# An earlier due time for the unit work that the eighth job's lists need

## The chip, the core and the metric

The kernel runs on one core of a Trainium2 chip. The metric is the device time in microseconds: the median of three runs, and beside it one execution taken by the hardware profiler. Engines are named as in the profile: PE is TensorE (PEld its weight loads), DVE is VectorE, ACT is ScalarE, POOL is GpSimd and SP is SyncE, which here only issues DMAs.

## What is computed

A gated recurrence runs along 4 sequences of 3648 steps with 256 channels, and a two-level mixture of experts with 16 experts (4 groups of 4) is applied to its 14592 output rows. Every row goes to exactly one expert.

```python
f = lower_bound + (1 - lower_bound) * sigmoid(f_logit)
h[t] = f[t] * h[t-1] + (1 - f[t]) * x[t]          # rows of h are the tokens
g = argmax(h @ w_group);  e = argmax(h @ w_expert[g])
out[row] = g_w * e_w * (relu(h[row] @ w1[g, e]) @ w2[g, e])   # 256 -> 1024 -> 256
```

`g_w` and `e_w` are the softmax weights of the chosen group and expert.

## The kernel before

**Units.** The rows are cut into 29 units of 512. A unit is loaded as one transfer (1 MB; on ScalarE's queue from unit 12 on, `p1_load`), goes through tanh and an affine map on ScalarE (`p1_ta`), a gate and two scans on VectorE (`p1_tb`), is transposed to row form on TensorE and copied out by ScalarE (`p1_back`), and its router products are made (`p1_router`, `p1_logits`). Units 8 to 27 are routed in groups of two: `route_thunks` finds each row's expert and place, and eight indirect DMAs on POOL scatter the group's rows to a list per expert in HBM (`xs`, line 393).

**Jobs.** Expert work comes as 32 jobs, numbered from 0 here. Job k (0 to 15, kind A) takes the first 2 to 5 blocks of 128 rows of an expert that is chosen while units are still being made: `EARLY[k]` says from which unit on (its cut) and how many blocks, and `choose` and `place` pick the expert and the rows' place. The eighth job is job 7, `EARLY[7] = (14, 3)`: 384 rows, from the lists as they stand when units 0 to 13 are in. Jobs 16 to 31 take what is left. The first four (`RAW = 4`) use the fp32 weights as loaded and work out their own output at once; later jobs split each weight piece into an fp16 and a bf16 part (a cast on ScalarE, line 971, and a difference on VectorE, line 973), and a job's second product stands behind the next job's first.

**Loads of a job.** Four weight pieces of 512 KB come on SyncE's queue (`job_weights`), up to eight staging buffers ahead; the rows come by `job_rows` (line 946), also on SyncE, and must wait until the scatters of all units before the cut have landed. `early_rows(u)` puts down the row loads of the jobs with cut u. SyncE works strictly in program order.

**What sets the order.** The work on units is a list of 577 small pieces, `thunks`. Job steps are written out one after the other, and after each step `bg_step` puts down as many pieces as a rate says. A step is a block of the first product or a part of the second: 10 per job for jobs 0 to 5, 19 for jobs 6 and 7, 20 for jobs 8 to 10. `due` holds pairs: by this step, this many pieces. The rate is the largest, over the open pairs, of pieces missing by steps left. The pair for job mi + 2 falls in the middle of job mi, so that of job 7 (piece 334, where `early_rows(14)` has been put down) falls in the middle of job 5, at step 55. SyncE, TensorE, VectorE and ScalarE are held to the order in which this is written, apart from what a scheduling layer moves within it; POOL's order is that layer's. In the functions below `thunks` come from `p1_thunks`, `macros` are the jobs, `marks[u]` is the number of pieces up to `early_rows(u)`.

Of the kernel before, what the change touches and what calls it, by code (L numbers as in the profile page):

```python
# [22 lines left out]
EARLY = [(4, 2), (6, 2), (8, 2), (8, 2), (10, 2), (10, 2), (12, 3), (14, 3),  # L23
         (16, 4), (18, 4), (20, 4), (22, 5), (24, 5), (26, 5), (28, 5), (28, 5)]
# [11 lines left out]
RAW = 4  # L36
# [17 lines left out]
def gated_scan_moe(ctx: ExitStack, tc, zx, lower, wroute, wexp, out, S):  # L54
# [785 lines left out]
    def make_job(kind, idx):  # L840
        j = Job()
        j.kind, j.idx = kind, idx
        j.len = EARLY[idx][1] * P if kind == "A" else CAPS[idx] if kind == "B" else P
        j.tiles = -(-j.len // P)
        j.chunks, j.pieces, j.cols, j.parts = [], [], [], []
        at = 0
        while at < j.len:
            rest = j.len - at
            if kind == "B":
                w = rest if rest <= UNIT else UNIT if rest >= UNIT + P else UNIT - P  # L850
            else:
                w = 2 * P if rest > 3 * P else P if rest > 2 * P else rest
            n = UNIT // w
            j.cols.append([list(range(c, min(KF, c + n))) for c in range(0, KF, n)])
            j.pieces += [(b, min(2 * P, at + w - b)) for b in range(at, at + w, 2 * P)]
            parts, b = [], at
            while b < at + w:
                m = at + w - b
                g = 1 if m > 64 else 2
                parts.append((b, min(m, P // g), g))  # L860
                b += P // g
            j.chunks.append((at, w))
            j.parts.append(parts)
            at += w
        j.raw = kind == "A" and idx < RAW
        j.wh, j.wl, j.st = {}, {}, {}
        j.hh, j.hl = {}, {}
        j.xh, j.xl = {}, {}
        return j
# [279 lines left out]
    macros = [[make_job("A", e)] for e in range(NE)]  # L1149
# [17 lines left out]
    def first_parts():  # L1167
        out = []
        for (j,), u in zip(macros, PLAN):
            half = {}  # L1170

            def begin(j=j, half=half):
                half[0] = bank("m2")
                raw2(j, 0, 0, range(KF // 2), half[0])
            fs = [lambda j=j: job_xt(j, 0)]
            fs += [lambda j=j, cs=cs: m1_step(j, 0, cs) for cs in j.cols[0]]
            fs += [begin, lambda j=j, half=half: m2_step(j, 0, 0, half[0])]
            out += [(u, f) for f in fs]
        return out

    thunks, marks = p1_thunks(list(range(NU)), GROUPS, first_parts())
# [56 lines left out]
    def work(mac):  # L1238
        return sum(len(j.chunks) * KF + sum(len(p) for p in j.parts) for j in mac)

    due = []
    at = 0
    for mi, mac in enumerate(macros):
        at += work(mac)
        if mi + 2 < len(macros):
            nxt = macros[mi + 2][0]
            due.append((at - (work(mac) // 2 if mi else 0), marks[EARLY[nxt.idx][0]] if nxt.kind == "A" else marks["order"]))
            if nxt.kind == "A" and nxt.idx >= NE - 2:
                due[-1] = (at - work(mac) // 2, marks["order"])
    now = [sum(work(mac) for mac in macros[:len(PLAN)])]  # L1250
    credit = [0.0]

# [110 lines left out]
```

## Time and profile before

| what | value |
|---|---|
| median of three runs | 763.11 us (760.62 to 766.0) |
| profiled execution | 761.96 us |
| its span, first to last instruction | 760.2 us |
| mean granted TensorE clock | 0.994 |
| TensorE busy | 715.6 us, 94% |
| VectorE busy | 514.6 us, 68% |
| ScalarE busy | 445.9 us, 59% |
| POOL busy | 296.3 us, 39% |
| bytes moved by DMA | 151.35 MB, 199 GB/s on average |

The shares are averages over stages that have different limits, so the stretch of the jobs in question is read from the views by window. A busy TensorE is not one at its peak. A wait is put down to the engine that released it last. A record of a queue (SPq, ACTq) is the issue of a DMA, not its transfer.

### The profile page before, as it was taken

Reading aid. Unit: us, or ns where it says so; the run is one execution under the profiler, and the core shown is the slowest. Engines: PE = TensorE matmul, PEld = TensorE weight load, DVE = VectorE, ACT = ScalarE, POOL = GpSimd, SP = SyncE. Lnnn points to the kernel's source line nnn. Section 1 sums busy time; section 2 is a strip of 40 time slices with the busy share of each in tenths; the row PEclk is TensorE's granted clock in tenths of the full one; section 3 lists DMA queues with packets and bytes.
Section 4 is the critical chain, followed back from the end, with each engine's and each line's share of the span. In section 5 each row is a group of like instructions: output and inputs, shape, how many; then the busy total and the mean of one; then the engine's idle time right before and its main releaser. Section 6 shows DMA issues by size and latency. Waiting matters only on the chain.

```text
span 760.2 us, 17863 instructions
## 1 busy us (share of the span) xinstructions
PE 715.6 (94%) x6471; PEld 588.0 (77%) x6471; DVE 514.6 (68%) x1086; ACT 445.9 (59%) x827; POOL 296.3 (39%) x314
## 2 busy tenths in 40 slices
PE   3569999998899999999999999999999999999995
PEld 1457888886788888888999676867778886777895
DVE  6899758999799976495556754644644645755660
ACT  6567767887577855454545644544544545655651
POOL 3656267668567764632222121312122121123232
PEclk9999999999999999999999999999999999999998
DMA  8978789989888873657994470617155345655520
GB/s 326 413 255 292 243 351 289 408 316 310 289 258 292 242 211 117 170 146 189 222 241 106 113 189 29 169 43 188 47 155 131 114 133 168 196 174 170 168 65 23
DMA packets 100410, 151.35 MB, mean 199 GB/s; under 512 B 60203, under 2 KB 70206, under 8 KB 97504
## 3 DMA queue, kind: packets, MB, share of 16 engines
q1 hardware_dynamic: 85792, 102.84, 46.1%
q0 software_dynamic: 11408, 30.02, 10.7%
q10 hardware_dynamic: 3120, 17.34, 6.7%
q8 instruction: 51, 0.84, 0.5%
q14 instruction: 39, 0.32, 0.1%
HBM read 112.49 MB, written 37.96 MB: 198 GB/s over the span
## 4 chain that ended last, share of the span: by engine, by line
PE 71%; DVE 11%; issue 8%; DMA 3%; POOL 3%; ACT 2%; another core or an unknown queue 1%; SPq 1%; POOLq 0%; DVEq 0%
PE ps_m L1129 28%; PE ps_m L1099 7%; PE ps_m L1097 7%; PE ps_m L1098 7%; PE ps_m L1110 4%; PE ps_m L1071 4%; PE ps_p L1097 3%; PE ps_p L1098 3%; PE ps_p L1099 3%; PE ps_p L284 3%; POOL out_dram L1143 3%; DVE h L256 2%; DVE w L973 1%; PE ps_p L303 1%; DVE hl L1103 1%
## 5 line engine op out<-in xcount | busy, mean ns | idle before, releaser
L1129 PE MATMUL ps_m<-w,hh 128*128 128x256 f16 (+5 forms) x1260 | 218.9, 268 | 1.3 <-issue 1.3
L1129 PE MATMUL ps_m<-w,hl 128*128 128x256 f16 (+4 forms) x740 | 188.5, 267 | 0.6 <-issue 0.6
L973 DVE TENSOR_TENSOR w<-st,w 128x1024 bf16<-128x1024 f32 x112 | 135.8, 1219 | 68.2 <-ACT w L971 66.7
L393 POOL DMA_INDIRECT xs<-rows,posi x114 | 138.2, 1212 | 87.6 <-ACT rows L288 25.6
L1143 POOL DMA_INDIRECT out_dram<-o,info x67 | 71.6, 1069 | 244.1 <-ACT o L1141 226.6
L1129 PE MATMUL ps_m<-w,rows 128*128 128x256 f16 (+5 forms) x880 | 133.8, 267 | 0.3 <-issue 0.3
L1129 PEld LDWEIGHTS <-hh 128*128 128x128 f16 (+7 forms) x1260 | 117.9, 101 | 15.6 <-issue 3.3
L971 ACT CAST w<-st 128x1024 f16<-128x1024 f32 x112 | 116.1, 1047 | 17.6 <-PE ps_m L1129 12.5
L1097 PE MATMUL ps_m<-xh,w 128*128 128x256 f16 (+9 forms) x494 | 120.4, 256 | 2.5 <-DVE hl L1103 2.4
L1099 PE MATMUL ps_m<-xh,w 128*128 128x256 f16 (+9 forms) x494 | 120.3, 256 | 0.8 <-issue 0.8
L1098 PE MATMUL ps_m<-xl,w 128*128 128x256 bf16 (+9 forms) x494 | 120.3, 256 | 0.0
L1103 DVE SCALAR_TENSOR_TENSOR hl<-ps_m,hh 128x512 bf16<-128x512 f32 (+7 forms) x107 | 71.1, 671 | 40.6 <-ACT hh L1102 24.7
L1098 PEld LDWEIGHTS <-w 128*128 128x128 f16 x800 | 78.3, 98 | 25.3 <-issue 3.7
L1097 PEld LDWEIGHTS <-w 128*128 128x128 f16 x800 | 78.3, 98 | 23.2 <-issue 1.6
L1099 PEld LDWEIGHTS <-w 128*128 128x128 bf16 x800 | 78.3, 98 | 22.8 <-issue 0.4
L1143 POOL DMA_INDIRECT out_dram<-o,meta x47 | 53.4, 1136 | 101.8 <-ACT o L1141 69.1
L1129 PEld LDWEIGHTS <-rows 128*128 128x128 f16 (+4 forms) x880 | 81.6, 101 | 10.0 <-issue 0.6
L1102 ACT ACTIVATE hh<-ps_m 128x512 f16<-128x512 f32 (+7 forms) x107 | 63.3, 594 | 37.1 <-PE ps_m L1099 32.1
L1141 ACT ACTIVATE o<-ps_m,info 128x256 f32<-128x256 f32 (+4 forms) x67 | 31.1, 463 | 91.5 <-PE ps_m L1129 75.8
L1129 PEld LDWEIGHTS <-hl 128*128 128x128 bf16 (+4 forms) x740 | 70.8, 101 | 9.1 <-issue 1.9
L256 DVE TENSOR_TENSOR_SCAN h<-zt,h 128x512 f32<-128x512 f32 (+3 forms) x48 | 56.6, 1191 | 0.5
L1103 DVE SCALAR_TENSOR_TENSOR hh<-ps_p,rows 128x512 bf16<-128x512 f32 (+7 forms) x30 | 17.6, 586 | 45.4 <-ACT rows L1102 45.3
(203 smaller groups left out, 1183.4 us busy)
## 6 DMA issues: line engine op xcount, KB each, us to landing
st<-in_wexp_dram SPq DMA_DIRECT2D x112, 512.0 KB
zt<-in_zx_dram ACTq DMA_DIRECT2D x16, 1024.0 KB
w<-in_wexp_dram SPq DMA_DIRECT2D x16, 512.0 KB
xs<-blank SPq DMA_DIRECT2D x26, 258.0 KB
zt<-in_zx_dram SPq DMA_DIRECT2D x6, 1024.0 KB
st<-in_zx_dram SPq DMA_DIRECT2D x8, 512.0 KB
xr<-xs SPq DMA_DIRECT2D x12, 258.0 KB
xr<-xs SPq DMA_DIRECT2D x16, 129.0 KB
```

The source lines that it names most:

```text
L256: sn = nc.vector.tensor_tensor_scan(out=h[:, k, c0 - a:c1 - a], data0=ff[:, k, c0 - a:c1 - a], data1=uu[:, k, c0 - a:c1 - a], initial=init ...
L393: sc = nc.gpsimd.indirect_dma_start(out=xs_v[G["t0"] + t][:, :], out_offset=bass.IndirectOffsetOnAxis(ap=R["posi"][:, t:t + 1], axis=0), i ...
L971: nc.scalar.copy(j.wh[i], j.st[i])
L973: nc.vector.tensor_tensor(out=j.wl[i], in0=j.st[i], in1=j.wh[i], op=ALU.subtract)
L1097: nc.tensor.matmul(po, w1_at(j.wh, k, c), xh[:, k], start=(k == 0), stop=False)
L1098: nc.tensor.matmul(po, w1_at(j.wh, k, c), xl[:, k], start=False, stop=False)
L1099: nc.tensor.matmul(po, w1_at(j.wl, k, c), xh[:, k], start=False, stop=(k == KD - 1))
L1102: eviction[0] = nc.scalar.activation(hi, pv, AF.Relu).ins
L1103: nc.vector.scalar_tensor_tensor(out=h_at(j.hl[ch], cs, slice(0, w)), in0=pv, scalar=0.0, in1=hi, op0=ALU.max, op1=ALU.subtract)
L1129: nc.tensor.matmul(pm[i * q:i * q + n, 0:dw], h_at(h[ch], [c], ts)[:, 0], w2_at(w, c)[:, i * dw:(i + 1) * dw], start=(c == 0 and s == 0), ...
L1141: nc.scalar.activation(o[s, 0:dw], pm[s, 0:dw], AF.Copy, scale=lt.bitcast(F32)[s, r, 1:2])
L1143: nc.gpsimd.indirect_dma_start(out=out_v[out_n[0]].rearrange("n (g d) -> (n g) d", g=g), out_offset=bass.IndirectOffsetOnAxis(ap=lt[s, r, ...
```

## The change

One line is added behind the loop that fills `due`: the pieces up to `early_rows(14)` (piece 334) are to be put down by the last step of job 3, step 40, and no longer by step 55.

```diff
             if nxt.kind == "A" and nxt.idx >= NE - 2:
                 due[-1] = (at - work(mac) // 2, marks["order"])
+    due.append((sum(work(mac) for mac in macros[:RAW]), marks[EARLY[RAW + 3][0]]))
     now = [sum(work(mac) for mac in macros[:len(PLAN)])]
```

No other pair is changed. Going through `bg_step` with the two lists gives the pieces put down by the end of each job (two units with their routing are 34 pieces):

| end of job | 0 | 1 | 2 | 3 | 4 | 5 | 6 | 7 | 8 | 9 | 10 |
|---|---|---|---|---|---|---|---|---|---|---|---|
| before | 210 | 247 | 279 | 301 | 319 | 341 | 380 | 415 | 450 | 484 | 515 |
| with the change | 212 | 252 | 293 | 334 | 346 | 362 | 392 | 422 | 454 | 485 | 515 |

The instructions themselves stay the same; their order on the engines moves. On SyncE before, at the row loads of job 7 (`posA_2055` is the place of its rows, the two `xr` loads are its rows; the two `st` loads ahead of them are the second and third weight piece of job 8):

```order
L963 DMA st_2210<-in_wexp_dram 128x1024
L963 ISA
L963 DMA st_2215<-in_wexp_dram 128x1024
L896 ISA
L896 TENSOR_LOAD posA_2055
L896 ISA x2
L946 ISA
L946 REGISTER_ALU
L946 DMA xr_2321<-xs 128x258
L946 ISA
L946 DMA xr_2323<-xs 128x516
```

With the change, the same two loads (now `posA_1952`, `xr_2126`, `xr_2128`) stand directly behind the choice of job 8's expert (`who_1922`), which follows the third weight piece of job 6; `st_2147` is the fourth piece of job 6:

```order
L661 TENSOR_LOAD who_1922
L661 ISA x2
L896 ISA
L896 TENSOR_LOAD posA_1952
L896 ISA x2
L946 ISA
L946 REGISTER_ALU
L946 DMA xr_2126<-xs 128x258
L946 ISA
L946 DMA xr_2128<-xs 128x516
L963 ISA
L963 DMA st_2147<-in_wexp_dram 128x1024
```

So these row loads moved ahead of eight weight loads. On POOL before, around the scatters of units 12 and 13 (`posi_1897`; the two `out_0_dram` rows are job 3's output, and the bookkeeping of units 14 and 15 begins at `sel_2383`):

```order
L393 DMA xs<-rows_1518,posi_1897 248832x258 x3
L1143 DMA out_0_dram<-o_1908,xr_1228 14592x256
L1143 DMA out_0_dram<-o_1938,xr_1228 14592x256
L393 DMA xs<-rows_1518,posi_1897 248832x258
L393 DMA xs<-rows_1651,posi_1897 248832x258 x4
L674 TENSOR_SCALAR sel_2383<-fill_2368,top_2370 128x16
L677 TENSOR_SCALAR gone_2385<-sel_2383 128x16
L393 DMA xs<-rows_1793,posi_2279 248832x258
```

With the change the scatters of units 12 and 13 read `posi_1854`, and the bookkeeping of units 14 and 15 (`sel_2211` and the four rows after it) and job 3's output stand as follows:

```order
L393 DMA xs<-rows_1506,posi_1854 248832x258 x4
L393 DMA xs<-rows_1636,posi_1854 248832x258 x2
L674 TENSOR_SCALAR sel_2211<-fill_2196,top_2198 128x16
L711 TENSOR_TENSOR got_2258<-got_2258,sel_1933 128x16
L677 TENSOR_SCALAR gone_2213<-sel_2211 128x16
L712 TENSOR_TENSOR taken_94<-taken_94,got_2258 128x16
L678 TENSOR_TENSOR least_96<-least_96,gone_2213 128x16
L393 DMA xs<-rows_1636,posi_1854 248832x258 x2
L1143 DMA out_0_dram<-o_2062,xr_1228 14592x256
L1143 DMA out_0_dram<-o_2089,xr_1228 14592x256
```

The last two of these scatters now stand behind that bookkeeping, and job 3's output stands behind all eight. Between job 1's second output write and the eighth of these scatters there are 19 scatters, 2 output writes and 3 such groups of bookkeeping; between job 1's second output and job 3's first there were 14 scatters before.

## Rows read from the trace of the kernel before

**Rows 1.** Busy time by stretch, all engines; the first line names the columns.

```profile
core 0: us, PE busy (x) PEld busy (x) DVE busy (x) ACT busy (x) POOL busy (x), PEclk, DMA share, GB/s
...
101.50:120.00 18.50, 18.50 (x129) 15.46 (x128) 11.81 (x26) 13.28 (x27) 12.45 (x13) 1.00 0.81 285
120.00:136.80 16.80, 16.80 (x103) 14.40 (x102) 13.67 (x32) 13.86 (x26) 11.74 (x16) 1.00 1.01 341
...
136.80:160.00 23.20, 23.20 (x260) 20.42 (x258) 23.10 (x49) 19.55 (x36) 12.30 (x11) 1.00 1.02 400
160.00:215.00 55.00, 48.96 (x507) 40.42 (x504) 49.16 (x99) 40.01 (x78) 41.33 (x42) 1.00 0.91 292
215.00:270.00 55.00, 53.84 (x535) 47.61 (x533) 54.23 (x105) 41.90 (x82) 40.34 (x39) 1.00 0.81 259
270.00:700.00 430.00, 428.08 (x3757) 344.67 (x3756) 254.33 (x494) 224.05 (x393) 110.69 (x109) 1.00 0.54 148
```

**Rows 2.** Waits of TensorE, 60 to 270 us: total, times, longest, in us.

```profile
PE ps_m L1097 <- DVE hl L1103: 2.1, 3, 1.0
PE ps_m L1129 <- issue: 1.9, 7, 0.4
PE ps_p L284 <- DVE both L381: 1.3, 1, 1.3
```

**Rows 3.** Timeline of TensorE: start, us, engine, line, operation.

```profile
101.50 0.59 PE L1071 MATMUL ps_m<-xh,w 128*128 128x256 f32 x2
...
103.23 0.60 PE L284 MATMUL ps_p<-ident,h 128*128 128x128 f32 x4
...
136.79 0.27 PE L1097 MATMUL ps_m<-xh,w 128*128 128x256 f16 x1
```

**Rows 4.** Groups of instructions on VectorE, 101.5 to 270 us: busy us, mean ns.

```profile
L256 DVE TENSOR_TENSOR_SCAN h<-zt,h 128x512 f32<-128x512 f32 (+3 forms) x30 | 34.0, 1140 | 0.2
...
L245 DVE SCALAR_TENSOR_TENSOR zt<-zt 128x1024 f32<-128x1024 f32 (+1 forms) x15 | 17.7, 1180 | 5.6 <-ACT zt L229 5.6
```

**Rows 5.** Timeline of VectorE, 155 to 175 us.

```profile
156.48 0.18 DVE L381 TENSOR_TENSOR both<-ps_p,both 128x32 f32<-128x32 f32 x1
...
159.62 1.28 DVE L256 TENSOR_TENSOR_SCAN h<-zt,h 128x512 f32<-128x512 f32 x1
...
167.91 0.31 DVE L330 TENSOR_REDUCE mx<-Lg 128x40 f32<-128x160 f32 x1
...
170.44 0.67 DVE L1103 SCALAR_TENSOR_TENSOR hl<-ps_m,hh 128x512 bf16<-128x512 f32 x1
```

**Rows 6.** POOL, the scatter group: 101.5 to 120 us, then 120 to 136.8 us.

```profile
L393 POOL DMA_INDIRECT xs<-rows,posi x8 | 8.5, 1058 | 5.7 <-DVE rows L375 2.0 <-issue 1.9 <-ACT rs L308 1.8
...
L393 POOL DMA_INDIRECT xs<-rows,posi x6 | 9.1, 1512 | 3.3 <-ACT rs L308 1.3 <-issue 0.9 <-DVE rows L375 0.8
```

**Rows 7.** Timeline of POOL, 100 to 160 us.

```profile
103.08 0.98 POOL L1143 DMA_INDIRECT out_dram<-o,xr  x1 [0.30 <-issue]
...
129.06 2.01 POOL L393 DMA_INDIRECT xs<-rows,posi  x1 [0.30 <-issue]
...
131.99 0.33 POOL L674 TENSOR_SCALAR sel<-fill,top 128x16 f32<-128x16 f32 x1 [0.91 <-DVE got L706]
...
133.92 1.81 POOL L393 DMA_INDIRECT xs<-rows,posi  x1 [0.81 <-DVE rows L375]
...
153.56 1.04 POOL L393 DMA_INDIRECT xs<-rows,posi  x1 [1.01 <-ACT rows L286]
```

**Rows 8.** Timeline of SyncE's DMA issues, 130 to 165 us.

```profile
137.41 0.93 SPq L946 DMA_DIRECT2D xr<-xs  x2
...
138.71 15.41 SPq L963 DMA_DIRECT2D st<-in_wexp_dram  x8
...
162.01 0.93 SPq L946 DMA_DIRECT2D xr<-xs  x2
```

**Rows 9.** Timeline of ScalarE, 148 to 156 us.

```profile
150.80 2.00 ACT L971 CAST w<-st 128x1024 f16<-128x1024 f32 x2
```

## The prediction

> **What bounds the kernel now.** I read the busy time by stretch first [rows 1]. From 101.5 to 160 us TensorE is busy all the time, from 160 to 215 it is idle for 6.0 us, from 215 to 270 for 1.2, and from 270 to 700 for 1.9 of 430. The granted clock is 1.00 in all stretches from 101.5 on, the higher of its two levels, so nothing is to be won or lost there. A change that only reorders work, and is back in step with the old order by the end of job 10, can win what TensorE waits in between: at most 6.0 + 1.2 = 7.2 us, 0.9% of the kernel.
>
> Who ends those waits is the second view [rows 2]: the largest are VectorE's (`hl` 2.1 us, `both` 1.3), and 1.9 us have no releaser that the trace shows. So behind the idle TensorE stands a full VectorE: busy 23.1 of 23.2 us from 136.8 to 160 and 54.2 of 55 from 215 to 270, while from 101.5 to 136.8 it has 11.8 + 13.7 = 25.5 of 35.3, 9.8 us free [rows 1]. That stretch is jobs 2 and 3: job 2's first product starts at 101.50, job 4's at 136.79 [rows 3]. The DMA engines are the other thing to look at: their share is 0.81, 1.01 and 1.02 in the three stretches from 101.5 to 160 [rows 1].
>
> **The change, part by part.** It adds one due time and no work. Emitting runs 5 pieces ahead of the old order at the end of job 1, 33 at the end of job 3, 21 after job 5, 12 after job 6, 7 after job 7 and none after job 10 (the table in the section on the change). Two units with their routing are 34 pieces, so the change carries nearly one group of two units out of jobs 4 to 10 and into the jobs before, 28 of 33 pieces into jobs 2 and 3. What a group costs:
>
> VectorE: per unit a gate of 1.18 us and two scans of 1.14, 3.46, twice 6.9 [rows 4]. Routing up to the running count goes from 167.91 to 170.44, 2.5 us; from there to the positions from 156.48 to 159.62, 3.1 less the one scan in it, 2.0 [rows 5]. Together 11.4 us; 28/34 of it is 9.4.
>
> TensorE: four transposes of `h` take 0.60 us as recorded [rows 3]; a unit has two such rows and the router's products, which I count as a third: 1.8, twice 3.6, on the high side since recorded ends overlap. It goes onto the path of jobs 2 and 3 and off it later, so it is zero in the sum, but those jobs end 28/34 of it, 3.0 us, later, at about 139.8.
>
> POOL: eight scatters, each 1.06 to 1.51 us and 0.30 of issue, 10.9 to 14.5 us [rows 6, 7].
>
> Do they fit in 35.3 + 3.0 = 38.3 us? VectorE needs 25.5 + 9.4 = 34.9, and has 3.4 left. POOL has 24.2 busy in 28 instructions [rows 1], with 0.30 each 32.6, and is given 28/34 of 10.9 to 14.5, that is 9.0 to 11.9: 41.6 to 44.5. POOL alone doesn't fit, by 3 to 6 us. VectorE at 91% in an in-order queue isn't safe either: where it is busy 49.2 of 55 us, from 160 to 215, TensorE waits for 6.0; where it is full, from 136.8 to 160, for nothing. So the new waits of TensorE in jobs 2 and 3 are between 0 and 4.2 (6.0 us in 55, over 38.3). I take 1.5, nearer to the stretch that lies beside it.
>
> The relief behind: VectorE sheds 12, 9, 5 and 3 pieces in jobs 4 and 5, 6, 7 and 8, at 11.4/34 = 0.34 us each 4.0, 3.0, 1.7 and 1.0. The first lies ahead of the waits, which begin with job 6 (161 us), and shortens the queue that VectorE enters it with. What this gives back is between 0 and 7.2 us; I take 3.5, half, because the waits of `both` are of TensorE and VectorE on one another, which a shorter queue does not shorten.
>
> What is moved past what, on SyncE. Row loads of job 7 now stand before the fourth weight piece of job 6 and all of job 7; before, they stood behind the third piece of job 8. SyncE is in order, so whatever keeps these row loads back keeps the weights back. They wait for the last scatter of units 12 and 13. In the order on POOL 19 scatters, three bookkeeping groups and two output writes lie between job 1's second write (start 103.08) and that scatter, and two of the scatters stand behind the bookkeeping of units 14 and 15, which needs VectorE's list of that group. From 104.1: 19 times 1.36 to 1.81, 25.8 to 34.4; two writes of 1.3; three groups of 1.1 (from 131.99 to the next scatter at 133.92, less its wait of 0.81) [rows 6, 7]: 135.8 to 144.4, and POOL's waits come on top (0.81 to 1.01 where the rows show one). I take 144. From a scatter's end to the row loads that wait for it the old trace has 6.3 us (131.07 to 137.41) and 7.4 (154.60 to 162.01), both under a full DMA; with fewer weights under way it can be shorter, above nothing. Row loads 144 to 151.4, weights 1.3 later (137.41 to 138.71) [rows 8]. The piece is 512 KB, at 400 GB/s 1.3 us, and at most as long as a scatter's 7.4: there at 146.6 to 160.1. It was used at 151.8, the second of the two casts from 150.80 [rows 9]; moved by the 3.0, less what job 4 no longer carries (6 pieces at 3.6/34, 0.6), at 154.2. So between 7.6 us early and 5.9 late; ScalarE would stand at the cast, and the evictions behind it that free TensorE's banks. I take 1.0.
>
> POOL's price is where a rule bears on it. The scatter group's mean is 1.06 us where VectorE is busy 11.8 of 18.5 us and 1.51 where it is busy 13.7 of 16.8 [rows 1, 6]. The Trainium skill, page "SBUF — State Buffer", section "Who interferes with whom", says that GpSimd and VectorE share one port pair as an exclusive lock, held for a whole instruction, and that VectorE instructions with two SBUF inputs contend with GpSimd's reads; that speaks against putting gates and splits beside scatters. By that rule the 19 scatters would all cost 1.51 us, the row loads would come near the late end, and the sum would have 5.9 where it has 1.0, 765.9; the trace agrees in direction, with two rows, and shows no mechanism.
>
> **Sum.** The profiled execution took 761.96 us (span 760.2 and 1.76 around it). 761.96 + 1.5 + 1.0 - 3.5 = 760.96. It lies 1.15 under the median 763.11 of the runs shown; against that the same sum gives 762.1. I forecast 761.5, between them.
>
> **Rivals.** A: as summed, a small shift that nearly cancels. For it: no engine gets less work in all, and TensorE works through the stretch either way.
>
> B: the shift empties VectorE's queue ahead of jobs 6 to 9 and all 7.2 us go, nothing new comes: 763.11 - 7.2 = 755.9. For it: the waits are VectorE's; against it: 1.9 of them are nobody's, and VectorE still holds over 90% of the stretch.
>
> C, on the other side: SyncE is held at job 7's row loads and job 6's fourth weight piece comes late. It decides from the point where the piece lands after 154.2: with a landing of 1.3 us that is a release of the row loads after 151.6, with one of 7.4 already after 145.5. Place: the casts of job 6, then job 7's pieces right behind. Price: 5.9 late for job 6, with nothing won back, 763.1 + 5.9 = 769.0; with 1.3 more for job 7's first piece behind it 770.3. For it: POOL doesn't fit, and the prefetch of eight staging buffers stands empty meanwhile; against it: the DMA engines are less full then, and the middle of the bounds is in time.
>
> D: nothing moves because TensorE hides it all: 763. For it: TensorE's zero idle from 101.5 to 160.
>
> **How the numbers follow.** A 0.45, B 0.18, C 0.25, D 0.12. About 1%, 7.6 us, is what a measurement of this kernel can tell from no change. Faster by more than that needs more than B holds in waits, so a third of B: 0.05. Slower needs C near its late end together with waits in jobs 2 and 3 (up to 4.2): half of C, 0.12. Within: 0.83. The range goes from B, 755.5, to C, 769.5; some 0.13 lies above it and 0.06 below.
>
> **What would show it.** In the changed kernel's trace: SyncE's two row loads of job 7 at 145 to 153, and then its weights, where the old trace has a run of eight weight issues from 138.71 on; a DMA share from 138 to 150 clearly under 1.0; POOL without gaps from 104 to 150; VectorE about 90% busy from 101.5 to 139.8. Right in A: TensorE's idle from 160 to 270 falls to about 4 us and 1 to 2 us of it appear before 140. Wrong if ScalarE waits for a weight load at job 6's casts by more than 3 us (C), if TensorE's waits from 160 on stay at 7 (no relief), or if anything behind job 10 differs by more than 1 us.

## The result, and the profile of the changed kernel

The change made the kernel slower by 1.4%: 774.08 us (median of six, 771.92 to 775.91) against 762.98 for the kernel before on the same chip, a ratio of 1.014 with a 95% interval of 1.0106 to 1.0174. That is 11.1 us, outside the range that was given. The profiled execution took 772.6 us, its span 770.8.

Busy time by stretch in the changed kernel, with the columns of [rows 1]:

```profile
core 0: us, PE busy (x) PEld busy (x) DVE busy (x) ACT busy (x) POOL busy (x), PEclk, DMA share, GB/s
101.50:136.80 35.30, 35.30 (x244) 29.33 (x243) 28.19 (x63) 26.02 (x52) 26.82 (x29) 1.00 0.90 305
136.80:160.00 23.20, 18.57 (x147) 14.68 (x146) 16.71 (x36) 14.53 (x28) 18.17 (x17) 0.85 0.86 301
160.00:215.00 55.00, 50.85 (x519) 43.47 (x517) 51.32 (x107) 41.95 (x79) 29.13 (x31) 0.97 0.90 314
215.00:270.00 55.00, 53.05 (x524) 46.45 (x522) 52.72 (x99) 43.48 (x80) 43.54 (x39) 1.00 0.86 274
270.00:700.00 430.00, 428.14 (x3773) 345.40 (x3776) 252.81 (x490) 221.84 (x389) 114.11 (x112) 1.00 0.53 146
```

From 101.5 to 136.8 TensorE is full, as in [rows 1]. The loss is in the second row: from 136.8 to 160, where TensorE had no idle time before, it is now idle for 4.6 us, and the granted clock is 0.85 of its upper level. From 160 to 270 it is idle for 6.1 us (before 7.2), so the relief that was to come there is 1.1 us. Behind 270 nothing moved: 428.14 busy against 428.08.

TensorE's waits from 101.5 to 215 us (total, times, longest), and its timeline around the largest:

```profile
PE ps_m L1129 <- ACT hh L1102: 3.8, 1, 3.8
PE ps_m L1097 <- DVE hl L1103: 2.9, 2, 1.9
```

```profile
148.32 0.64 PE L1033 MATMUL ps_p<-ident,xr 128*128 128x128 f32 x4
152.76 1.04 PE L1129 MATMUL ps_m<-w,hh 128*128 128x256 f16 x4 [3.80 <-ACT hh L1102]
153.58 0.42 PE L1097 MATMUL ps_m<-xh,w 128*128 128x256 f16 x1
```

TensorE waits 3.8 us for the first eviction of job 4's first product, that is for ScalarE to copy it out of TensorE's accumulators (`hh`). Behind the wait a matmul of 256 columns takes 0.42 us where [rows 3] has 0.27: the clock has fallen to 1.2 GHz. Why the eviction is late stands in ScalarE's timeline, and in the chain of work that ended last (start, us, what):

```profile
139.99 0.34 ACTq L205 DMA_DIRECT2D zt<-in_zx_dram  x1
140.37 1.06 ACT L219 ACTIVATE zt<-zt 128x1024 f32<-128x1024 f32 x1 [3.00 <-DMA st<-in_wexp_dram]
...
151.16 1.06 ACT L219 ACTIVATE zt<-zt 128x1024 f32<-128x1024 f32 x1 [4.59 <-DMA zt<-in_zx_dram]
152.12 0.58 ACT L1102 ACTIVATE hh<-ps_m 128x512 f16<-128x512 f32 x1
```

```profile
129.47 10.50 DMA st<-in_wexp_dram
...
139.99 11.15 DMA zt<-in_zx_dram
```

ScalarE stands for 4.59 us at the tanh of unit 19, whose load of 1 MB was issued at 139.99 and landed 11.15 us later; the eviction is the next instruction in its queue. The issue itself had waited for the landing of a weight piece that took 10.50 us. So the chain that sets the end goes through 21.65 us of transfers in a row, where that of the kernel before stays on TensorE until 147.76. SyncE's DMA issues in the same time, and the share of the DMA engines from 130 to 160 us:

```profile
139.38 2.13 SPq L963 DMA_DIRECT2D st<-in_wexp_dram  x4
156.83 1.05 SPq L946 DMA_DIRECT2D xr<-xs  x2
158.15 0.33 SPq L963 DMA_DIRECT2D st<-in_wexp_dram  x1
```

```profile
130.00:140.00 10.00, 10.00 (x67) 8.55 (x66) 9.73 (x27) 5.18 (x11) 7.57 (x8) 1.00 0.98 283
140.00:150.00 10.00, 8.13 (x74) 6.46 (x72) 6.54 (x19) 5.46 (x12) 7.40 (x9) 1.00 0.99 349
150.00:160.00 10.00, 7.24 (x42) 5.69 (x43) 7.21 (x11) 8.84 (x15) 8.17 (x7) 0.66 0.71 255
...
101.50:146.06 44.56, 43.73 (x314) 36.10 (x313) 33.86 (x83) 31.23 (x64) 33.04 (x35) 1.00 0.91 304
151.60:158.40 6.80, 5.64 (x27) 4.24 (x28) 4.95 (x6) 6.80 (x11) 5.58 (x5) 0.50 0.65 242
```

SyncE is held at job 7's row loads until 156.83, as rival C had it, and issues no weight from 141.5 to 158. But the DMA engines are full without it until 150. Full does not mean that they move as much. In the kernel before the same stretches are:

```profile
130.00:140.00 10.00, 10.00 (x75) 8.52 (x74) 8.73 (x24) 8.40 (x16) 7.67 (x9) 1.00 1.01 402
140.00:150.00 10.00, 10.00 (x104) 8.84 (x102) 9.90 (x18) 8.11 (x15) 5.89 (x6) 1.00 1.03 409
...
101.50:136.52 35.02, 35.02 (x227) 29.59 (x226) 25.20 (x58) 26.86 (x52) 23.91 (x28) 1.00 0.91 311
```

By the clock the changed kernel moves no more bytes here but fewer: 10.8 MB from 101.5 to 136.8 us (before 11.0) and 7.0 MB from there to 160 (before 9.3), each the rate times the time. What has grown is what had moved by a given place in the program: the second product of job 3 ends at 146.06 and not at 136.52, and from 101.5 to that place 13.5 MB moved and not 10.9.

The span grew by 10.6 us (770.8 for 760.2). The rows account for about 8.0 of them: 4.6 of idle time up to 160, 2.8 because 5.64 busy us ran at half the clock from 151.6 to 158.4, 1.7 at a clock of 0.97 from 160 to 215, less the relief of 1.1. The rest was not followed.

### The profile page after: what moved, and what is told of

Its sections match the earlier page's. It is cut to its first block, busy times and chain, and to the rows that moved or that the text cites. A ratio compares the mean times of both kernels' runs of the same rounds, so it can differ in the third digit from the quotient of the medians.

```text
span 770.8 us, 17856 instructions
## 1 busy us (share of the span) xinstructions
PE 719.2 (93%) x6467; PEld 589.4 (76%) x6471; DVE 515.9 (67%) x1086; ACT 447.1 (58%) x827; POOL 300.5 (39%) x314
## 3 DMA queue, kind: packets, MB, share of 16 engines
q0 software_dynamic: 11408, 30.02, 10.6%
## 4 chain that ended last, share of the span: by engine, by line
PE 61%; issue 13%; DVE 11%; DMA 5%; POOL 4%; ACT 3%; SPq 1%; another core or an unknown queue 1%; POOLq 0%; ACTq 0%; DVEq 0%
PE ps_m L1129 26%; PE ps_m L1099 7%; PE ps_m L1097 6%; PE ps_m L1098 6%; POOL out_dram L1143 4%; PE ps_m L1110 3%; DVE w L973 3%; PE ps_p L1099 3%; PE ps_p L1097 2%; DMA zt<-in_zx_dram 2%; PE ps_p L1098 2%; DVE h L256 2%; PE ps_m L1071 2%; PE ps_p L284 2%; DVE hl L1103 2%
## 5 line engine op out<-in xcount | busy, mean ns | idle before, releaser
L1097 PE MATMUL ps_m<-xh,w 128*128 128x256 f16 (+9 forms) x494 | 122.3, 259 | 5.8 <-DVE hl L1103 3.5
L1099 PE MATMUL ps_m<-xh,w 128*128 128x256 f16 (+9 forms) x494 | 122.2, 259 | 0.1
L1098 PE MATMUL ps_m<-xl,w 128*128 128x256 bf16 (+9 forms) x494 | 122.2, 259 | 0.1
```

Of the source, the lines that this page charges most:

```text
L1097: nc.tensor.matmul(po, w1_at(j.wh, k, c), xh[:, k], start=(k == 0), stop=False)
L1098: nc.tensor.matmul(po, w1_at(j.wh, k, c), xl[:, k], start=False, stop=False)
L1099: nc.tensor.matmul(po, w1_at(j.wl, k, c), xh[:, k], start=False, stop=(k == KD - 1))
```

## Experiments

The runs were taken on several chips, so each is held against the kernel before on its own chip (751.8 to 762.5 us there); ratios have 95% intervals. Names that begin with e_ and a_ are the changed kernel with an edit, names with b_ the kernel before with one.

### Four single waits: e_swap, e_warm, e_rows, e_load

The trace suggests four single causes, and each run takes one away.

**e_swap**: the tanh of unit 19 behind job 4's second eviction.

```diff
-(p1_load(u + AHEAD - 1), u + 1 in us and p1_ta(u + 1))
+(p1_load(u + AHEAD - 1), u + 1 in us and (later.append(u + 1) if u + 1 == 19 else p1_ta(u + 1)))
 def bg_step(q, left, n):
+    if later and now[0] + n >= 44:
+        with tc.issue_after(eviction[0]):
+            p1_ta(later.pop())
```

> The changed kernel, but the tanh of unit 19, which waits 4.6 us on ScalarE for its load at 151.16 us, is put behind the second eviction of job 4's first product, not ahead of the first. No work changes, and no load. Theory L (this one wait on ScalarE's in-order queue, with job 4's evictions behind it, is the loss, together with the clock that falls behind it): TensorE's wait of 3.8 us before 152.76 goes, and the half clock of 151.6 to 158.4 with it (about 3.4 us), so about 774.1 - 7 = 767. Theory S (SyncE is held at job 7's row loads and weights come late): the weights are as late as before, 773 to 775. Theory F (VectorE, GpSimd and the DMA engines are simply overfull there): the wait moves to the next eviction or to VectorE, 772 to 775.

**e_warm**: 64 idle matmuls in TensorE's gap, behind the third block of job 4's first product.

```diff
+if j.kind == "A" and j.idx == RAW and cs[0] == 4:
+    with tc.issue_after(mm.ins):
+        warmed[0] = keep_warm(bank("m2"), 64)
```

> The changed kernel with 64 matmuls of 128 columns whose result nobody reads, put on TensorE into the gap of 3.8 us behind the third first product of job 4. They take some 3.5 to 4 us at the higher clock where TensorE stood idle. This asks how much of the loss is the clock. If the fall of the granted clock behind the gap is a price of its own: the clock stays at 1.00 from 151 to 158, and 774.1 - 3.4 = 770.7. If something else (evictions, VectorE, loads) binds in that stretch: the clock stays up, and the time stays at 773 to 775. If the matmuls outlast the gap: up to 1 us longer.

**e_rows**: job 7's row loads back in SyncE's queue where they stood before.

```diff
 def early_rows(u):
+    if u == EARLY[RAW + 3][0] and now[0] < 56:
+        later.append(u)
+        return
...
 now[0] += n
+if later and now[0] >= 56:
+    early_rows(later.pop())
```

> The changed kernel, but job 7's two row loads are put into SyncE's queue at the place in job 5 at which they stood before the change; the units and everything else stay as early as the change has them. Theory S (rival C of the prediction: SyncE held at the row loads, weights behind them late): weights flow from 140 us on, and the most of the 11 us goes, 763 to 767. Theory L (the late load ahead of tanh on ScalarE): that load comes no sooner, since more weights now share the DMA engines with it; the wait of 4 to 5 us at tanh stays, 772 to 776.

**e_load**: the loads of z and x most of a unit earlier.

```diff
-seq += [lambda u=u: p1_back(u - 1, 0)]
+seq += [lambda u=u: (p1_back(u - 1, 0), p1_load(u + AHEAD))]
```

> The changed kernel, but each unit's load of z and x on ScalarE's queue is issued most of a unit earlier (behind the first copy of the unit two before in place of one step later); same bytes, same buffers. Theory L: the loads land ahead of their tanh, ScalarE's wait of 4.6 us goes with TensorE's 3.8 and the clock's fall, 766 to 769. Theory F (the DMA engines are full, so an earlier load makes another one late): weights or row loads come later by as much, 771 to 775. Theory S: nothing of SyncE's order changes, 772 to 775.

| kernel | us | ratio to the kernel before |
|---|---|---|
| changed kernel | 774.08 | 1.0140 (1.0106 to 1.0174) |
| e_swap | 772.96 | 1.0139 (1.0075 to 1.0203) |
| e_warm | 775.96 | 1.0174 (1.0112 to 1.0236) |
| e_rows | 772.11 | 1.0142 (1.0092 to 1.0192) |
| e_load | 779.99 | 1.0262 (1.0200 to 1.0323) |

None brings back anything that these intervals can tell, and e_load costs 1.2% more. (In e_load 172 of VectorE's and 97 of TensorE's rows moved too, so that price is not the loads' alone.) The waits of TensorE in e_swap, 101.5 to 215 us, show why:

```profile
PE ps_p L316 <- ACT w L973: 2.4, 1, 2.4
PE ps_p L303 <- ACT rows L286: 1.6, 1, 1.6
PE ps_m L1112 <- ACT hl L1076: 1.3, 1, 1.3
```

The 3.8 us are gone and three other waits, 5.3 us together, have come. In e_warm the stretch from 136.8 to 160 keeps the full clock, and TensorE still has 3.95 us without work, beside the 64 matmuls that do nothing:

```profile
136.80:160.00 23.20, 19.25 (x206) 15.92 (x205) 16.80 (x35) 14.96 (x28) 16.68 (x17) 1.00 0.83 289
```

So the fallen clock is not what binds there. In e_rows SyncE issues twelve weights from 137.24 on with no row load between them, and ScalarE waits for the same load a little longer than in the changed kernel:

```profile
137.24 34.90 SPq L966 DMA_DIRECT2D st<-in_wexp_dram  x12
...
150.50 1.06 ACT L219 ACTIVATE zt<-zt 128x1024 f32<-128x1024 f32 x1 [5.64 <-DMA zt<-in_zx_dram]
```

That is the end of rival C (theory S): SyncE was held as it says, and its release is worth nothing that can be told. Theory L falls too, as far as it names one wait. Where each wait that goes is replaced by another, a resource that all of them share may be short. Theory D: the DMA engines are full there, and the change asks for the loads, scatters and row loads of about two units earlier. Theory E, against it: the order of the work on the engines, which the change moves as well.

### Bytes alone: b_dma, b_dma1, b_dmalate

The kernel before, with copies of 1 MB that nobody reads on SyncE's queue: three in jobs 2 and 3 (b_dma, below), one there (b_dma1: at step 28 alone), or three in jobs 11 and 12 (b_dmalate: at steps 158, 174 and 190). In b_dma and b_dma1 the order of every engine but SyncE stays as it was up to 400 us; in b_dmalate 77 of VectorE's and 45 of ScalarE's rows move, from 330 us on. SyncE runs ahead of the other engines: the copies of b_dma were issued at 95.90, 120.14 and 136.59 us.

```diff
 now[0] += n
+for k, at in enumerate((22, 28, 34)):
+    if now[0] - n < at <= now[0]:
+        sync.dma_start(out=idle[k * P:(k + 1) * P, 0:2048], in_=zx[k * P:(k + 1) * P, :])
```

> The kernel before, with three copies of 1 MB from zx to a scratch tensor that nobody reads, put into SyncE's queue in jobs 2 and 3 (3 MB, about what the change carries into the stretch: two loads of z and x, and eight scatters). No engine gets any work. Theory D (the DMA engines are full from 120 to 200 us, so traffic put there ahead of its time makes everything behind it late): 3 MB at the 300 to 400 GB/s of that stretch are 7.5 to 10 us, so 762 + 7 to 10 = 769 to 772, and TensorE's idle appears from 140 us on. Theory E (what counts is the order of work on VectorE, ScalarE and GpSimd): 762 to 764.

> The kernel before with one copy of 1 MB, in the middle of jobs 2 and 3, in place of three. Theory D with no room left: a third of the 8.0 us, 2.7, so 765. Theory D with some room before it binds: less than 1 us, 762 to 763.5.

> The kernel before with the same three copies of 1 MB to a scratch tensor, but put into SyncE's queue in jobs 11 and 12 (about 270 to 340 us), where the DMA engines' share is 0.55. Theory D (the stretch is full, the bytes cost because they stand there): nothing, 762 to 763.5. If such copies cost wherever they stand (by SyncE's queue or the landing that later loads wait for): 766 to 771, as in jobs 2 and 3.

| kernel | us | before, same chip | ratio |
|---|---|---|---|
| b_dma, 3 MB in jobs 2 and 3 | 770.52 | 762.50 | 1.0105 (1.0081 to 1.0129) |
| b_dma1, 1 MB there | 761.68 | 756.91 | 1.0067 (1.0039 to 1.0095) |
| b_dmalate, 3 MB in jobs 11 and 12 | 757.23 | 756.91 | 1.0001 (0.9973 to 1.0029) |

3 MB of copies with no work for any engine cost the kernel before 8.0 us, within the 7 to 10 that theory D gave. A single copy costs 0.67%, 4.8 us and not a third of 8 (its interval goes from 3 to 7), so there was no room at that place. The same 3 MB cost nothing later, where the kernel before has a DMA share of 0.54. ScalarE's timeline and a stretch of b_dma:

```profile
129.44 1.04 ACT L972 CAST w<-st 128x1024 f16<-128x1024 f32 x1 [2.68 <-DMA st<-in_wexp_dram]
...
139.80 1.04 ACT L972 CAST w<-st 128x1024 f16<-128x1024 f32 x1 [1.08 <-DMA st<-in_wexp_dram]
142.87 1.05 ACT L972 CAST w<-st 128x1024 f16<-128x1024 f32 x1 [1.17 <-DMA st<-in_wexp_dram]
```

```profile
101.50:136.80 35.30, 33.38 (x217) 27.95 (x216) 25.37 (x59) 24.31 (x48) 22.52 (x27) 1.00 0.96 327
```

Here it is the weights that come late, and TensorE is idle for 1.9 us already before 136.8. The copies stand on SyncE's own queue, ahead of these weights, while the loads and scatters that the change moves are issued by ScalarE and POOL. So the runs show what 3 MB cost at this place, and not that the change's own transfers cost it in the same way.

### Half the change: e_half

```diff
-due.append((sum(work(mac) for mac in macros[:RAW]), marks[EARLY[RAW + 3][0]]))
+due.append((sum(work(mac) for mac in macros[:RAW]), marks[EARLY[RAW + 3][0]] - 16))
```

> The change at half its size: the same due place, 16 pieces fewer (318 of the pieces by the end of the first four jobs, where the kernel before has 301 and the changed one 334). Theory D: half the traffic is moved, 5 us of the 11: 766 to 769. If the loss comes from a point that is passed only near the full size (one load that comes later than its reader): 761 to 765.

770.60 us, 1.0095 (1.0071 to 1.0120): with 17 of the 33 pieces moved, two thirds of the loss and a little more than the 766 to 769 us of theory D. The loss does not come only near the full size.

### Bytes taken away: a_halfw and b_halfw, a_quart and b_quart

Both kernels without every second weight load of jobs 4 to 7 (4 MB), or with the first of four alone (6 MB less); the splits are kept. Up to 400 us the order of all engines but SyncE is that of the kernel that was cut.

The edit is in `job_weights`; for the 6 MB it reads `and i:` and `j.st[0]`.

```diff
+if j.kind == "A" and 4 <= j.idx < 8 and i % 2:
+    j.st[i] = j.st[i - 1]
+    return
 st = stg.tile([P, 1024], F32, name="st")
```

> The changed kernel, but of jobs 4 to 7 every second weight piece is not loaded; its split into two halves reads the piece before it again (so these jobs compute with wrong weights, with the same instructions on every engine). It takes 4 MB of 512 KB loads out of the stretch from 110 to 190 us. To be held against the same cut in the kernel before. Theory D (full DMA engines): the loads of z and x and the row loads land sooner, TensorE's wait of 3.8 us and the fall of the clock go, and the kernel is within 4 us of the kernel before with the same cut: 760 to 767. Theory E (order on the engines): still 9 to 11 us behind the kernel before with the same cut, 770 to 774.

> The kernel before with the same cut: of jobs 4 to 7 every second weight piece is not loaded and the piece before it is read again (wrong weights in these jobs, same instructions). The control of the run above. TensorE waited for 6.0 us between 160 and 215 us there, of which a part may hang on loads: both theories 757 to 763.

> The changed kernel, of whose jobs 4 to 7 only the first of the four weight pieces is loaded and read four times (wrong weights there, the same instructions on every engine): 6 MB out of the stretch, where 4 MB took the distance to the kernel before with the same cut from 11.6 to 3.6 us. If the 3.6 are still DMA: 763 to 764 (within 1.5 of the control). If they are something else, as the eight evictions and splits that stand behind more work of the units on VectorE: 766 to 767, as with 4 MB out.

> The kernel before with the same cut of 6 MB, the control of the run above. With 4 MB out it was at 762.8, no faster than whole. All theories: 761 to 763.5.

| cut | changed kernel | kernel before | distance |
|---|---|---|---|
| none | 1.0140 (1.0106 to 1.0174) | 1 | 1.4%, 11.1 us |
| 4 MB | 1.0054 (1.0035 to 1.0074) | 1.0009 (0.9986 to 1.0031) | 0.45%, 3.6 us |
| 6 MB | 1.0069 (1.0044 to 1.0093) | 0.9981 (0.9954 to 1.0009) | 0.88%, 7.0 us |

The kernel before gains nothing that can be told by having 4 or 6 MB less to load; the changed kernel gains half of its loss or more. With 6 MB out it gains no more than with 4. Fewer weights also leave less for SyncE to hold back, but e_rows takes that hold away with all bytes kept, and gains nothing that can be told. The tanh that waited 4.59 us, in a_quart:

```profile
140.63 0.33 ACTq L205 DMA_DIRECT2D zt<-in_zx_dram  x1
...
146.74 1.06 ACT L219 ACTIVATE zt<-zt 128x1024 f32<-128x1024 f32 x1 [0.31 <-DMA zt<-in_zx_dram]
147.70 0.58 ACT L1105 ACTIVATE hh<-ps_m 128x512 f16<-128x512 f32 x1
```

The load takes about 6.1 us and not 11.15, is there nearly in time, and the eviction comes 4.4 us sooner. The expectation for a_quart on theory D alone, a distance of at most 1.5 us, did not hold. Of the 11.1 us the two pairs leave 3.6 and 7.0: 4 to 7.5 us go with the bytes, the rest is something else.

### The rest: a_split to b_both, a_qearly and b_qearly

With the loads cut, TensorE's remaining waits are for VectorE (`hl`, 5.0 us in 4). So I left out splits, with all loads (a_split, b_split) and with the 6 MB cut (a_both, b_both); the edit is in `job_split`.

```diff
 if j.raw:
     return
+if j.kind == "A" and 4 <= j.idx < 8 and i:
+    j.wh[i], j.wl[i] = j.wh[0], j.wl[0]
+    return
```

> The changed kernel; of jobs 4 to 7 all weight pieces are loaded, but only the first of four is split, and its halves serve for all four (wrong weights there). Takes twelve casts of 1.0 us off ScalarE and twelve subtractions of 1.15 us off VectorE between 125 and 190 us, and no byte off the DMA engines. To be held against b_split. If the whole loss were the full DMA engines: still 9 to 11 us (1.2 to 1.4%) behind b_split. If VectorE's and ScalarE's queues are the rest of the loss (about 5 us): 5 to 7 us behind it (0.7 to 0.9%).

> The kernel before with the same twelve splits left out, the control of a_split. TensorE's waits for VectorE between 160 and 215 us may shrink: up to 6 us faster than the kernel before, 0 to 0.8%.

> The changed kernel; of jobs 4 to 7 only the first weight piece is loaded and only it is split (wrong weights there): 6 MB off the DMA engines and twelve operations each off VectorE and ScalarE. To be held against b_both. If DMA engines and the two queues together are the loss: within 2 us of b_both (0 to 0.25%). If there is a third cause (GpSimd's scatters, the order on TensorE): 4 us or more (0.5%) behind it.

> The kernel before with the same loads and splits left out, the control of a_both: as b_split, 0 to 0.8% faster than the kernel before.

a_split 1.0137 (1.0103 to 1.0172), b_split 1.0148 (1.0109 to 1.0188), a_both 1.0093 (1.0058 to 1.0129), b_both 1.0119 (1.0087 to 1.0151). The four can't be read as they were meant: the control b_split lost 12 us with 24 instructions less. The splits are known to the layer that deals the engines' queues, and without them it dealt these anew: in b_split nearly 200 of TensorE's rows and as many of VectorE's stand elsewhere than in the kernel before. What the pair does show is how much an order is worth here, with no byte added, and in b_both with 6 MB less. From b_split:

```profile
136.80:160.00 23.20, 19.53 (x170) 15.52 (x169) 14.69 (x29) 14.86 (x30) 8.30 (x9) 0.85 1.02 412
```

TensorE is idle for 3.7 us in the stretch where it had no idle time before, with VectorE, ScalarE and POOL a third idle or more.

The second try takes a_quart and b_quart, keeps all their work and moves job 5's four splits, in the loop over the jobs (the layer then moved 117 and 78 of TensorE's rows as well). In the changed kernel they stand among job 4's four evictions on VectorE; in the kernel before three stood ahead of the first eviction and the fourth ahead of the second.

```diff
-q.extend(prep_thunks(j))
+q.extend(prep_thunks(j)[4 if mi == RAW else 0:])
+if mi == RAW - 1:
+    q.extend(prep_thunks(macros[RAW + 1][0])[:4])
```

> The changed kernel with 6 MB of weight loads left out (as a_quart: of jobs 4 to 7 only the first weight piece is loaded, wrong weights there), and the four splits of job 5 put down one job earlier, so that on VectorE job 4's four evictions follow one another and the splits fill VectorE's waits in the routing ahead of them. No work and no bytes change against a_quart. If the 3.6 to 6.9 us that a_quart is behind its control are VectorE's splits among the evictions: they shrink to under 2 us (ratio to the kernel before 0.998 to 1.001). If they are anything else: 1.004 to 1.009 as a_quart.

> The kernel before with the same 6 MB left out and the same four splits of job 5 one job earlier: the control. There two of the four stood ahead of job 4's evictions already. 0.996 to 1.002 of the kernel before.

a_qearly 1.0058 (1.0045 to 1.0071), b_qearly 1.0009 (0.9999 to 1.0018): a distance of 0.49%, 3.8 us. The place of the splits is not the cause of what is left; whether a part of the 7.0 us went with it the intervals don't tell. TensorE's waits from 101.5 to 215 us in a_qearly, and the stretch:

```profile
PE ps_m L1100 <- DVE hl L1106: 4.0, 4, 1.8
PE ps_p L355 <- DVE scn L348: 2.4, 1, 2.4
```

```profile
136.80:160.00 23.20, 18.99 (x175) 16.53 (x174) 21.97 (x48) 17.56 (x36) 18.36 (x19) 1.00 0.72 243
```

The clock stays up, and the DMA engines have room (0.72). VectorE is busy 22.0 of 23.2 us, and TensorE is idle for 4.2. The wait has only moved, in part from the evictions to the routing (`scn`). That the 3.8 us are a full VectorE is what these rows suggest; no run that takes work off VectorE without dealing the queues anew was made, so it is not shown. The order of the work (theory E) stays a rival. In a_both VectorE has 8.6 us free in this stretch and the DMA engines are not full, and TensorE is idle for 4.9 us all the same, behind ScalarE:

```profile
136.80:160.00 23.20, 18.30 (x141) 15.31 (x140) 14.58 (x32) 11.16 (x25) 14.11 (x16) 0.87 0.79 249
```

And where the load comes in time, job 4's first eviction still stands late in its queue. In b_quart it starts 1.7 us behind job 4's first matmul:

```profile
136.85 0.27 PE L1100 MATMUL ps_m<-xh,w 128*128 128x256 f16 x1
138.52 0.60 ACT L1105 ACTIVATE hh<-ps_m 128x512 f16<-128x512 f32 x1
```

In a_quart it starts 6.5 us behind, at 147.70, since two outputs of job 3, the first of which waits for TensorE, and the tanh stand ahead of it:

```profile
141.23 0.27 PE L1100 MATMUL ps_m<-xh,w 128*128 128x256 f16 x1
144.98 0.47 ACT L1144 ACTIVATE o<-ps_m,xr 128x256 f32<-128x256 f32 x1 [2.30 <-PE ps_m L1113]
```

No run moves these evictions alone.

## Why the prediction was wrong

**What bounds the kernel.** Right as a description, and misread. The DMA share of 1.01 and 1.02 stood in the first part ("the other thing to look at"), and no term of the sum came of it. I counted the moved work on VectorE, TensorE, POOL and SyncE, and not its bytes: two loads of 1 MB, the scatters and the row loads. This is the step that failed: a term that was put at nothing, and that the runs put at 4 to 7.5 of the 11.1 us (a_halfw and a_quart against their controls). By the rows that I had, 3 MB at 300 to 400 GB/s are 7.5 to 10 us, and b_dma measures 8.0; that this is near the whole loss is in part luck, since 3.6 to 7.0 us stay when bytes are taken away. What these are is open: a full VectorE, or the order of the work on the queues. TensorE's zero idle from 101.5 to 160 hid it: nothing waited for the DMA engines, so I took them for free of price where they were only just in time. The Trainium skill, page "DMA: Bandwidth & Descriptors", section "Issuing engines are not separate DMA queues", says that DMAs of different engines run on the same 16 DMA engines and interleave. The runs agree: with fewer weights on SyncE's queue the load of 1 MB on ScalarE's took about 6.1 us and not 11.15.

**The clock.** That "nothing is to be won or lost there" held only as long as TensorE was not idle: behind its wait of 3.8 us the granted clock was 0.50 for 6.8 us. It was no price of its own, since e_warm kept the clock up there and won nothing.

**Each queue that is moved past.** I followed SyncE's and POOL's and left out ScalarE's, on which the units' loads are issued and tanh waits for them, with job 4's evictions behind. It is where the changed kernel's loss shows (4.59 and 3.8 us), but e_swap says that it is the place and not the cause: without that wait others came.

**New waits of TensorE, 1.5 us (0 to 4.2), in jobs 2 and 3.** There are none until 136.8, and 4.6 from there to 160. With the DMA engines relieved 2.6 to 4.2 are left, by the profile most of it for VectorE. That these lie within the bound is luck, since they came from another place: the sum filled VectorE's 9.8 free us from 101.5 to 136.8 with 9.4 of work, and it took on 2.7 (28.19 for 25.48). What it left free lies above all in waits of the routing; these are VectorE's waits from 101.5 to 136.8 in the changed kernel:

```profile
DVE both L381 <- issue: 2.2, 1, 2.2
DVE sm L362 <- ACT ex L427: 1.8, 1, 1.8
DVE mx L330 <- ACT Lg L317: 0.9, 1, 0.9
```

What did not fit came after job 4 had begun, and jobs 2 and 3 ended at 146.1 us and not at about 139.8.

**Relief, 3.5 us.** 1.1. The idle from 160 to 270 went from 7.2 to 6.1, and a clock of 0.97 from 160 to 215 takes 1.7 back.

**Rival C, SyncE.** The mechanism took place, later than worked out: row loads at 156.83 where I had 145 to 153, the scatters that they wait for ending at 151.97; POOL's bookkeeping ahead of those alone waited 1.81 us for VectorE. Its price is nothing that can be told (e_rows). My forecast of a DMA share "clearly under 1.0" from 138 to 150, which was to come from it, was wrong: 0.99 from 140 to 150. The end of the range that stood for C was 769.5; and the 0.12 for slower were there for a cause that does not cost.

**POOL.** By my working from the Trainium skill's rule on the shared port (page "SBUF — State Buffer", section "Who interferes with whom") all scatters would have taken 1.51 us. The trace does not bear out that size: they took 1.24 from 101.5 to 120, 1.46 to 136.8, and 1.25 to 160. It agrees in direction, as the two rows of before do: the longest stand where VectorE is fullest (13.92 of 16.80 us, against 14.27 of 18.50 and 16.71 of 23.20). That the last scatter ended at 151.97, where I took 144, is not their length. The count began 2.7 us later, with job 1's second write at 105.77 and not at 103.08, and the last bookkeeping went from 145.43 to the scatter at 149.64, where I had 1.1 us for it:

```profile
105.77 0.98 POOL L1143 DMA_INDIRECT out_dram<-o,xr  x1 [0.30 <-issue]
...
145.43 0.33 POOL L674 TENSOR_SCALAR sel<-fill,top 128x16 f32<-128x16 f32 x1 [1.81 <-DVE got L706]
...
149.64 1.05 POOL L393 DMA_INDIRECT xs<-rows,posi  x1 [0.16 <-DMA zt<-in_zx_dram]
151.00 0.97 POOL L393 DMA_INDIRECT xs<-rows,posi  x1 [0.30 <-issue]
```

**Behind job 10.** Right: from 270 to 700 TensorE's busy time differs by 0.06 us.

## What to carry to other kernels

A change that moves work ahead moves its transfers too: where the DMA share is at 1.0, add up the moved bytes, divide by the rate of that stretch, and put the result into the sum, also when no engine waits for a transfer. A share near 1.0 does not say how much is moved: here it went with 283 GB/s and with 409. Whether a resource that nobody waits for has room can be asked directly, by an idle load of it at that place and the same load elsewhere. When each wait that an experiment removes is replaced by another, stop looking for the one wait and look for what they share. A sum of an engine's work over a stretch says nothing of where in its queue the one instruction stands for which the next engine waits.

## What the runs showed that I had not expected

- One copy of 1 MB, put on SyncE in jobs 2 and 3, cost 0.67% (0.39 to 0.95); three of them where the share is 0.54 cost nothing.
- A load on ScalarE's queue was issued only when a weight piece of SyncE's queue had landed: ScalarE waited 3.00 us for it, and the chain has the two transfers end to end (10.50 and 11.15 us).
- The granted clock fell to 1.2 GHz for 151.6 to 158.4 us, behind 3.8 us of idle TensorE. Filling the gap with idle matmuls kept 2.4 GHz and gave no time back.
- Taking 24 instructions out of the kernel before made it 12 us slower, with no byte added and a new order of the queues.
